# Attention decode on one core: the product with V turned to 512 moving columns in four column tiles

## The chip, the cores and the metric

The kernel runs on one core of a Trainium2 chip. The metric is the device time of one execution in microseconds (us), as the median of several executions. The time before is 677.42 us (677.16 to 677.44). A profiled execution has a span of its own, about 2 us shorter than the time.

The engines are TensorE (PE in the profile; PEld are its weight loads), VectorE (DVE), ScalarE (ACT), GpSimd (POOL) and SyncE (SP), which issues nearly all transfers. Sixteen DMA engines move the data.

## The reference

One decode step for two sequences: layer norm, 32-head attention over a cache of 8192 keys, a residual, and a gated feed-forward block. Nearly all bytes are the two caches, 134 MB each.

```python
q = (layernorm(x) @ wq)                        # 2 sequences, 32 heads, 128 wide
scores = einsum("bhqd,bhkd->bhqk", q, k) * 128 ** -0.5
p = softmax(scores)
o = einsum("bhqk,bhkd->bhqd", p, v)            # this product is what is changed
h = x + o @ wo
out = h + reglu(layernorm(h))                  # W_up, W_gate, W_down
```

## The kernel before

The work goes in 32 "pairs": one pair is two heads of one sequence. A pair has a 4 MB tile of K and a 4 MB tile of V, each 128 partitions by 128 key columns (index `j`) by 128. Head 0 sits on partitions 0 to 63, head 1 on 64 to 127. Two slots hold K tiles and two hold V tiles, so a tile is asked for two pairs ahead, as soon as its slot is free.

Scores of key columns 0 to 95 are made on VectorE (multiply, then a tree of additions), in two parts of 48. Columns 96 to 127 are transposed on TensorE, copied out by ScalarE and multiplied with q on TensorE. ScalarE takes the exponentials. Then `pv` multiplies with V:

```python
def pv(p):
    v_t = tile((2 * p + 1) % 4)
    ...                                        # cut: column of the result, waits on older batches
    for ci, (ei, j0, j1) in enumerate(parts):
        pe.wait(t_exp[p][ei], (sem_vl[ci], 16) if p == NP - 1 else t_v[p])
        for j in range(j0, j1):
            i = nc.tensor.matmul(
                Op[k % 2][:, col:col + 2], lhsT=v_t[:, j, :], rhs=e_t[p % 2][:, j, :],
                start=(nmm == 0), stop=(nmm == J - 1))
            nmm += 1
    t_pv[p] = pe.run(i)
```

V is the stationary operand, 128 x 128 for each `j`, and the two columns of exp weights (one for each head, zero on the other head's partitions) move. That is 128 weight loads and 128 matmuls a pair.

The loop over pairs, cut:

```python
for p in range(NP):
    for c in range(NCH):                       # the two VectorE parts
        dve.wait(t_k[p])                       # K tile has landed, on all DMA engines
        ...                                    # cut: multiply, tree of adds
        if c == 0:
            pe.wait(t_k[p])
            ...                                # cut: transposes, copies, score matmuls, exp
    sp.wait(*t_kfree[p])                       # both engines have read the K tile
    t_k[p + 2] = load(s, slot[s][:], kv(A_k_cache, p + 2))
    pv(p)
    load_v(p + 2)                              # waits for t_pv[p]
```

At the end `pv(30)`, the normalization of pairs 24 to 30, most of the output projection and then `pv(31)` follow. The last V tile arrives in four parts, and 48 matmuls of `pv(31)` wait for its late parts. After them come scale, the last of the output projection and the feed-forward block.

The softmax here doesn't subtract the row's maximum and nothing guards it: scores larger than these inputs give would overflow.

## Time and profile before

| | before |
|---|---|
| time, us | 677.42 |
| span of the profiled run, us | 675.6 |
| busy, us: PE / DVE / ACT | 294.0 / 493.6 / 202.0 |
| moved | 281 MB at 417 GB/s |
| instruction packets in the TensorE queue (q8) | 51 |

First the head of the page of the kernel before: busy time by engine, then the span in 40 slices (DMA row: mean busy share of the 16 engines in tenths), then the queues (packets, MB, share of the time of 16 engines).

```profile
PE 294.0 (44%) x6596; PEld 266.2 (39%) x6596; DVE 493.6 (73%) x428; ACT 202.0 (30%) x523; POOL 1.7 (0%) x11
...
DMA  9999999999999999999999999999999999999993
GB/s 373 433 434 370 430 426 432 427 430 428 434 427 430 430 434 429 432 434 427 424 428 430 431 432 434 429 432 430 426 429 428 431 428 433 428 430 392 418 411 117
...
q1 hardware_dynamic: 15872, 281.06, 97.9%
q8 instruction: 51, 0.84, 0.5%
q14 instruction: 9, 0.07, 0.0%
```

An instruction packet is one transfer that brings part of the program itself to an engine; q8 carries TensorE's (51 packets, 0.84 MB, so 16 KB each), q14 those of other engines.

No compute engine is close to full, and the DMA row is full until the last slice. Next the costly groups of the same page: line, engine, operation, tiles, count, then busy us and mean ns of one, then the idle time before and what ended it.

```profile
L366 DVE TENSOR_TENSOR prod<-slot,q_b 128x6144 bf16<-128x6144 bf16 x64 | 214.9, 3358 | 132.3 <-DMA slot<-in_A_k_cache_dram 131.1
L334 PE MATMUL O<-e,slot 128*128 128x2 bf16 x4096 | 118.7, 165 | 239.2 <-DMA slot<-in_A_v_cache_dram 119.8
L334 PEld LDWEIGHTS O<-e,slot 128*128 128x128 bf16 x4096 | 114.6, 104 | 243.5 <-ACT e L267 122.0
```

VectorE waits 131.1 us for K tiles. The chain of waits of the kernel before shows their rhythm. Its columns are the start, the length and what it was; start plus length is when a K tile had landed, and every second tile shows.

```profile
165.97 27.69 DMA slot<-in_A_k_cache_dram
...
204.81 27.86 DMA slot<-in_A_k_cache_dram
...
243.83 29.06 DMA slot<-in_A_k_cache_dram
...
284.06 27.70 DMA slot<-in_A_k_cache_dram
```

They land at 193.66, 232.67, 272.89 and 311.76 us, so 39.0, 40.2 and 38.9 us apart.

The end of the kernel before, from its timeline (start, length, engine, what, then the idle time before it and what ended it):

```profile
648.23 3.55 PE L334 MATMUL O<-e,slot 128*128 128x2 bf16 x128
...
664.30 1.44 PE L334 MATMUL O<-e,slot 128*128 128x2 bf16 x48 [1.55 <-DMA slot<-in_A_v_cache_dram]
```

The first line is a whole pair's PV, 3.55 us. The second is the 48 matmuls that wait for the last V part; TensorE idled 1.55 us before them, and 11.3 us of dependent work follow.

### The profile page before, as it was taken

The numbers are of one execution on the slowest core, as the hardware profiler recorded it, in microseconds if no ns is written. First come the engines' busy times: TensorE is split into PE (matmuls) and PEld (weight loads), VectorE is DVE, ScalarE is ACT, GpSimd is POOL, SyncE is SP. The second block draws the span as 40 slices with busy tenths as digits, with TensorE's granted clock in tenths as the row PEclk, the third lists the DMA queues.
The fourth block names the chain that finished last, engine by engine and source line by source line (L and its number), as shares of the span: only waits on it lengthen the run. The fifth ranks groups of instructions, "written<-read, shape, count | busy, mean of one in ns | idle before, by whom it ended". The sixth has DMA issues, their size and how long they took to land.

```text
span 675.6 us, 14430 instructions
## 1 busy us (share of the span) xinstructions
PE 294.0 (44%) x6596; PEld 266.2 (39%) x6596; DVE 493.6 (73%) x428; ACT 202.0 (30%) x523; POOL 1.7 (0%) x11
## 2 busy tenths in 40 slices
PE   2552254344445424443533444353344644334446
PEld 2442244333434423443433444343344534334335
DVE  1774577788777768877767887776788767778891
ACT  0630322233333223333312333331233332223330
POOL 1000000000000000000000000000000000000000
PEclk9955655566655566556556556555556555556555
DMA  9999999999999999999999999999999999999993
GB/s 373 433 434 370 430 426 432 427 430 428 434 427 430 430 434 429 432 434 427 424 428 430 431 432 434 429 432 430 426 429 428 431 428 433 428 430 392 418 411 117
DMA packets 15936, 281.97 MB, mean 417 GB/s; under 512 B 1442, under 2 KB 6916, under 8 KB 7044
## 3 DMA queue, kind: packets, MB, share of 16 engines
q1 hardware_dynamic: 15872, 281.06, 97.9%
q8 instruction: 51, 0.84, 0.5%
q14 instruction: 9, 0.07, 0.0%
q10 hardware_dynamic: 4, 0.00, 0.0%
HBM read 281.05 MB, written 0.00 MB: 416 GB/s over the span
## 4 chain that ended last, share of the span: by engine, by line
DMA 73%; DVE 24%; PE 1%; issue 1%; SPq 0%; DVEq 0%
DMA slot<-in_A_k_cache_dram 69%; DVE prod L366 15%; DVE tb L374 5%; DMA slot<-in_A_v_cache_dram 4%; DVE prod L374 3%; DVE scores L381 1%; PE S L473 0%; PE O L515 0%; PE O L334 0%; SPq L353 0%; SPq L135 0%; SPq L428 0%; PE W L473 0%; PE O L473 0%; PE W L309 0%
## 5 line engine op out<-in xcount | busy, mean ns | idle before, releaser
L366 DVE TENSOR_TENSOR prod<-slot,q_b 128x6144 bf16<-128x6144 bf16 x64 | 214.9, 3358 | 132.3 <-DMA slot<-in_A_k_cache_dram 131.1
L334 PE MATMUL O<-e,slot 128*128 128x2 bf16 x4096 | 118.7, 165 | 239.2 <-DMA slot<-in_A_v_cache_dram 119.8
L334 PEld LDWEIGHTS O<-e,slot 128*128 128x128 bf16 x4096 | 114.6, 104 | 243.5 <-ACT e L267 122.0
L397 ACT ACTIVATE kT<-T 128x1024 bf16<-128x1024 bf16 x128 | 126.5, 1022 | 170.6 <-PE T L391 169.7
L391 PE MATMUL T<-ident,slot 128*128 128x128 bf16 x1024 | 122.6, 306 | 77.5 <-DMA slot<-in_A_k_cache_dram 75.2
L374 DVE TENSOR_TENSOR tb<-prod 128x3072 bf16<-128x3072 bf16 (+1 forms) x128 | 148.2, 1158 | 4.4
L391 PEld LDWEIGHTS T<-ident,slot 128*128 128x128 bf16 x1024 | 99.7, 141 | 80.5 <-DMA slot<-in_A_k_cache_dram 78.2
L267 ACT ACTIVATE e<-scores 64x48 bf16<-64x48 f32 x128 | 32.8, 256 | 253.2 <-DVE scores L381 251.6
L374 DVE TENSOR_TENSOR prod<-tb 128x1536 bf16<-128x1536 bf16 (+1 forms) x128 | 84.2, 658 | 4.4
L259 PE MATMUL S<-qT,kT 128*128 128x2 bf16 x1024 | 48.2, 168 | 39.0 <-ACT kT L397 37.8
L259 PEld LDWEIGHTS S<-qT,kT 128*128 128x128 bf16 x1024 | 40.8, 107 | 57.6 <-ACT kT L397 57.6
L381 DVE TENSOR_REDUCE scores<-prod 128x48 f32<-128x384 bf16 x64 | 35.4, 553 | 2.2
L267 ACT ACTIVATION_READ_ACCUMULATOR e<-scores 64x1 f32 x128 | 23.6, 185 | 0.0
L267 ACT ACTIVATE e<-S 64x32 bf16<-64x32 f32 x64 | 12.9, 202 | 15.0 <-PE S L259 14.2
L267 ACT ACTIVATION_READ_ACCUMULATOR e<-S 64x1 f32 x64 | 12.9, 201 | 0.7
L212 DVE CAST qT<-W 128x64 bf16<-128x64 f32 x1 | 0.2, 225 | 12.0 <-PE W L207 12.0
L241 ACT ACTIVATE q_b<-O 128x512 bf16<-128x512 f32 x8 | 4.3, 595 | 15.6 <-PE O L236 15.6
L309 PE MATMUL W<-O_sb,X 128*128 128x2 bf16 (+1 forms) x136 | 5.0, 172 | 7.0 <-DVE O_sb L297 7.0
L309 PEld LDWEIGHTS W<-O_sb,X 128*128 128x128 bf16 x136 | 4.8, 118 | 7.2 <-DVE O_sb L297 7.2
L207 PE MATMUL W<-xlT,X 128*128 128x2 bf16 x128 | 3.6, 165 | 8.6 <-DMA X<-in_A_wq_dram 8.6
L207 PEld LDWEIGHTS W<-xlT,X 128*128 128x128 bf16 x128 | 3.5, 104 | 8.7 <-DMA X<-in_A_wq_dram 8.7
L285 DVE TENSOR_REDUCE zr<-O 128x16 f32<-128x48 f32 (+1 forms) x4 | 0.8, 204 | 8.3 <-PE O L277 8.3
(58 smaller groups left out, 39.3 us busy)
## 6 DMA issues: line engine op xcount, KB each, us to landing
slot<-in_A_k_cache_dram SPq DMA_DIRECT2D x32, 4096.0 KB, 27.8
slot<-in_A_v_cache_dram SPq DMA_DIRECT2D x31, 4096.0 KB, 32.2
X<-in_A_wq_dram SPq DMA_DIRECT2D x1, 4096.0 KB, 12.4
X<-in_A_wo_dram SPq DMA_DIRECT2D x1, 4096.0 KB, 49.1
slot<-in_A_v_cache_dram SPq DMA_DIRECT2D x1, 1536.0 KB, 21.5
slot<-in_B_W_up_dram SPq DMA_DIRECT2D x1, 1376.0 KB, 9.8
slot<-in_B_W_gate_dram SPq DMA_DIRECT2D x1, 1376.0 KB, 16.4
slot<-in_A_v_cache_dram SPq DMA_DIRECT2D x1, 1280.0 KB, 24.1
```

What stands on the lines that cost most here:

```text
L207: i = nc.tensor.matmul(Wp[:, h * B:(h + 1) * B], lhsT=wq[:, c, h * Dh:(h + 1) * Dh], rhs=lT[:, c * B:(c + 1) * B], start=(c == 0), stop=(c ...
L241: t_cp[m] = act.run(nc.scalar.activation(out=q_b[:, m * 512:(m + 1) * 512], in_=Op[m % 2][:], func=ACT.Copy))
L259: i = nc.tensor.matmul(Sp[p % 2][:, 2 * jj:2 * jj + 2], lhsT=kT[n % 3][:, k * 128:(k + 1) * 128], rhs=qT[:, 2 * p:2 * p + 2], start=True, ...
L267: t = act.run(nc.scalar.activation(out=e_t[p % 2][q, j0:j0 + nj, a], in_=src(q, a), func=ACT.Exp, scale=inv_sqrt_dh, accum_out=zs[q, 2 * p ...
L285: dve.run(nc.vector.tensor_reduce(out=zr[:, 2 * p0:2 * p1], in_=zbank(k)[:, 64:64 + n * (NCH + 1)].rearrange("p (n k) -> p n k", k=NCH + 1 ...
L309: i = nc.tensor.matmul(Wp[:, c * B + b0:c * B + b1], lhsT=wo_m[:, h, c, :], rhs=Ov[:, h // 2, h % 2, b0:b1], start=first[0], stop=last, sk ...
L334: i = nc.tensor.matmul(Op[k % 2][:, col:col + 2], lhsT=v_t[:, j, :], rhs=e_t[p % 2][:, j, :], start=(nmm == 0), stop=(nmm == J - 1))
L366: t_dm = dve.run(nc.vector.tensor_tensor(out=prod[:], in0=k_t[:, c * JC:(c + 1) * JC, :], in1=qv, op=ALU.mult))
L374: dve.run(nc.vector.tensor_tensor(out=o, in0=cur[:, :, 0:half], in1=cur[:, :, half:w], op=ALU.add))
L381: t_s = dve.run(nc.vector.tensor_reduce(out=sc[:], in_=cur, axis=AX.X, op=ALU.add))
L391: i = nc.tensor.transpose(Tp[n % 3][:, k * 128:(k + 1) * 128], k_t[:, j, :], ident[:])
L397: t_ev[n] = act.run(nc.scalar.activation(out=kT[n % 3][:], in_=Tp[n % 3][:], func=ACT.Copy))
```

## The change

The intent: swap the operands. Eight columns of exp weights (four key columns of two heads) become the stationary operand, and four key columns of V, 512 wide, move. That makes 32 matmuls a pair instead of 128. They go in turn to four column tiles of the array, which can work side by side. The result is an 8 x 512 block in each tile, of which only the "diagonal" blocks (exp column of `j` with V of the same `j`) are wanted. ScalarE copies the bank to fp32 memory, and four small fp32 matmuls with a selection matrix add the wanted blocks. The last pair keeps the old form.

```diff
-                        for j in range(j0, j1):
+                        ...                    # last pair: as before
+                        for j in range(j0, j1, VJ):           # VJ = 4
+                            g = 32 * (nmm % 4)
                             i = nc.tensor.matmul(
-                                Op[k % 2][:, col:col + 2], lhsT=v_t[:, j, :], rhs=e_t[p % 2][:, j, :],
-                                start=(nmm == 0), stop=(nmm == J - 1))
+                                o[g:g + 2 * VJ, :], lhsT=e_t[p % 2][:, j:j + VJ, :].rearrange("p j a -> p (j a)"),
+                                rhs=v_t[:, j:j + VJ, :].rearrange("p j d -> p (j d)"),
+                                start=(nmm < 4), stop=(nmm >= J // VJ - 4))
                             nmm += 1
...
+                def collect(p):                # run in the next pair, after its first exp
+                    act.wait(t_pv[p])
+                    ...
+                    t_os[p] = act.run(nc.scalar.activation(out=os_sb[:], in_=Op[p % 2][:], func=ACT.Copy))
+                    ...
+                    for jj in range(VJ):
+                        i = nc.tensor.matmul(
+                            Ob[:, 2 * p:2 * p + 2], lhsT=os_sb[:, jj * Dh:(jj + 1) * Dh],
+                            rhs=sel[:, 2 * jj:2 * jj + 2], start=(jj == 0), stop=(jj == VJ - 1))
...
-        Tp = [ps(f"T{i}", [128, GT * 128], BF16) for i in range(3)]
+        Tp = [ps(f"T{i}", [128, GT * 128], BF16) for i in range(2)]
...
+                            if p == NP - 1 and c == 1 and w == Dh // 2:
+                                t_O[3] = normalize(3, 24, 31, t_batch[3], False)
```

Cut here: the selection matrix built on GpSimd, the zeroing of the two banks, and the bookkeeping of batches. The results need a bank of their own (`Ob`), so the transposes give one up. The normalization of pairs 24 to 30 moves into VectorE's work of the last pair.

More of the change, by code (lines that the diff above doesn't have):

```diff
@@ L66, in bass_sequential_preLN__gqa_block_cached__glu_gated_reglu__decode_kernel @@
     FR = F - 10 * 128
+    VJ = 4
     eps = 1e-5
@@ L126, in bass_sequential_preLN__gqa_block_cached__glu_gated_reglu__decode_kernel @@
         o_c = sb("o_c", [128, B * DC], BF16)
-        Tp = [ps(f"T{i}", [128, GT * 128], BF16) for i in range(3)]
+        os_sb = sb("os_sb", [128, 512], F32)
+        sel = sb("sel", [128, VJ * 2], F32)
+        Tp = [ps(f"T{i}", [128, GT * 128], BF16) for i in range(2)]
         Sp = [ps(f"S{i}", [128, 512], F32) for i in range(2)]
         Op = [ps(f"O{i}", [128, 512], F32) for i in range(2)]
+        Ob = ps("Ob", [128, 512], F32)
         Wp = ps("W", [128, 512], F32)
@@ L166, in _ @@
                 pool.run(nc.gpsimd.memset(onesn[:], 1.0 / D))
+                pool.run(nc.gpsimd.memset(sel[:], 0.0))
+                for c in range(4):
+                    pool.last()
+                    pool.run(nc.gpsimd.tensor_copy(
+                        out=sel[32 * c:32 * c + 2 * VJ, :], in_=ident_f[0:2 * VJ, 0:2 * VJ]))
+                pool.last()
                 for e in e_t:
@@ L242, in _ @@
                         out=q_b[:, m * 512:(m + 1) * 512], in_=Op[m % 2][:], func=ACT.Copy))
+                dve.wait(t_cp[NP // 4 - 2], t_cp[NP // 4 - 1])
+                for o in Op:
+                    t_zero = dve.run(nc.vector.memset(o[:], 0.0))
                 t_pt, t_ev, t_sc, t_pv = {}, {}, {}, {}
+                t_os, t_ob = {}, {}
                 t_exp = {}
@@ L272, in zbank, with zcol @@
                 def zbank(k):
-                    return Sp[0] if k == 4 else Op[k % 2]
+                    return Sp[0] if k == 4 else Ob
+                def zcol(k):
+                    return 64 if k == 4 else 2 * NP
                 def z_sum(k, p0, p1):
@@ L277, in z_sum @@
                     t = pe.run(nc.tensor.matmul(
-                        zbank(k)[:, 64:64 + (p1 - p0) * 2 * (NCH + 1)], lhsT=ones_f[:],
+                        zbank(k)[:, zcol(k):zcol(k) + (p1 - p0) * 2 * (NCH + 1)], lhsT=ones_f[:],
                         rhs=zs[:, 2 * p0:2 * p1, :], start=True, stop=True))
@@ L286, in normalize @@
                         out=zr[:, 2 * p0:2 * p1],
-                        in_=zbank(k)[:, 64:64 + n * (NCH + 1)].rearrange("p (n k) -> p n k", k=NCH + 1),
+                        in_=zbank(k)[:, zcol(k):zcol(k) + n * (NCH + 1)].rearrange("p (n k) -> p n k", k=NCH + 1),
                         axis=AX.X, op=ALU.add))
@@ L296, in o_scale @@
                 def o_scale(k, p0, p1):
+                    src = Op[1][:, 0:2] if k == 4 else Ob[:, 2 * p0:2 * p1]
                     return dve.run(nc.vector.tensor_tensor(
-                        out=O_sb[:, 2 * p0:2 * p1], in0=Op[k % 2][:, 0:2 * (p1 - p0)], in1=zi[:, 2 * p0:2 * p1],
+                        out=O_sb[:, 2 * p0:2 * p1], in0=src, in1=zi[:, 2 * p0:2 * p1],
                         op=ALU.mult))
@@ L323, in pv @@
                     v_t = tile((2 * p + 1) % 4)
-                    k = next(kk for kk, (a, b_) in enumerate(batches) if a <= p < b_)
-                    col = 2 * (p - batches[k][0])
+                    o = Op[p % 2]
                     parts = vparts if p == NP - 1 else (
                         [(0, NCH * JC, J)] + [(1 + c, c * JC, (c + 1) * JC) for c in range(NCH)])
-                    if p == batches[k][0] and k >= 2:
-                        pe.wait(t_O[k - 2])
+                    pe.wait(t_zero)
+                    if p >= 2:
+                        pe.wait(t_os[p - 2])
                     nmm = 0
@@ L332, in pv @@
                         pe.wait(t_exp[p][ei], (sem_vl[ci], 16) if p == NP - 1 else t_v[p])
-                        for j in range(j0, j1):
+                        if p == NP - 1:
+                            for j in range(j0, j1):
+                                i = nc.tensor.matmul(
+                                    o[:, 0:2], lhsT=v_t[:, j, :], rhs=e_t[p % 2][:, j, :],
+                                    start=(nmm == 0), stop=(nmm == J - 1))
+                                nmm += 1
+                            continue
+                        for j in range(j0, j1, VJ):
+                            g = 32 * (nmm % 4)
                             i = nc.tensor.matmul(
-                                Op[k % 2][:, col:col + 2], lhsT=v_t[:, j, :], rhs=e_t[p % 2][:, j, :],
-                                start=(nmm == 0), stop=(nmm == J - 1))
+                                o[g:g + 2 * VJ, :], lhsT=e_t[p % 2][:, j:j + VJ, :].rearrange("p j a -> p (j a)"),
+                                rhs=v_t[:, j:j + VJ, :].rearrange("p j d -> p (j d)"),
+                                start=(nmm < 4), stop=(nmm >= J // VJ - 4))
                             nmm += 1
                     t_pv[p] = pe.run(i)
-                    if p + 1 in ends and p < NP - 1:
+                def collect(p):
+                    act.wait(t_pv[p])
+                    if p >= 1:
+                        act.wait(t_ob[p - 1])
+                    t_os[p] = act.run(nc.scalar.activation(out=os_sb[:], in_=Op[p % 2][:], func=ACT.Copy))
+                    k = next(kk for kk, (a, b_) in enumerate(batches) if a <= p < b_)
+                    pe.wait(t_os[p])
+                    if p == batches[k][0] and k >= 1:
+                        pe.wait(t_O[k - 1])
+                    for jj in range(VJ):
+                        i = nc.tensor.matmul(
+                            Ob[:, 2 * p:2 * p + 2], lhsT=os_sb[:, jj * Dh:(jj + 1) * Dh],
+                            rhs=sel[:, 2 * jj:2 * jj + 2], start=(jj == 0), stop=(jj == VJ - 1))
+                    t_ob[p] = pe.run(i)
+                    if p + 1 in ends:
                         t_batch[k] = z_sum(k, *batches[k])
@@ L361, in _ @@
                         dve.wait(t_k[p])
-                        if p == 0 and c == 0:
-                            dve.wait(t_cp[NP // 4 - 1])
                         dve.last()
@@ L386, in _ @@
                                 n = p * NG + g
-                                if n >= 3:
-                                    pe.wait(t_ev[n - 3])
+                                if n >= 2:
+                                    pe.wait(t_ev[n - 2])
                                 for k in range(GT):
@@ L391, in _ @@
                                     i = nc.tensor.transpose(
-                                        Tp[n % 3][:, k * 128:(k + 1) * 128], k_t[:, j, :], ident[:])
+                                        Tp[n % 2][:, k * 128:(k + 1) * 128], k_t[:, j, :], ident[:])
                                 t_pt[n] = pe.run(i)
@@ L397, in _ @@
                                 t_ev[n] = act.run(nc.scalar.activation(
-                                    out=kT[n % 3][:], in_=Tp[n % 3][:], func=ACT.Copy))
+                                    out=kT[n % 3][:], in_=Tp[n % 2][:], func=ACT.Copy))
                                 if g >= 1:
@@ L406, in _ @@
                                 NCH * JC, JP)
+                            if p == NP - 1:
+                                pv(p - 1)
+                            if p >= 1:
+                                collect(p - 1)
                         act.wait(t_s)
@@ L434, in _ @@
                             B_W_down[0:10 * 128].rearrange("(r p) n -> p r n", p=128)).then_inc(sem_wd, 16)
-                pv(NP - 2)
-                t_O[3] = normalize(3, 24, 31, t_batch[3], False)
                 pe.wait(t_O[3])
```

## The prediction

> **What bounds the kernel now.** The DMA queue. In the page's slices the 16 DMA engines are at least 90% busy in every slice but the last; 281 MB move at 417 GB/s over a 675.6 us span. In the chain of waits K tiles land 38.9 us apart for two pairs: 19.43 us per pair of 4 MB K and V tiles, 432 GB/s. VectorE (73% busy) waits 131.1 us for K tiles, about 4 us a pair; TensorE (44%) and ScalarE (30%) wait for VectorE or DMA. The queue is deep: by the list of DMA issues a V tile lands 32.2 us after its issue, against 9.7 us for moving one. So a V slot may come free some 20 us later (estimate: 32.2 less a tile or so) before the queue runs dry.
>
> **What the change does to TensorE.** PV is now 128 matmuls a pair with 2 moving columns: in the timeline 80 in 2.27 us and 48 in 1.44 us, 3.7 us. After: 32 matmuls of 512 columns. The 128-column transposes run 8 in 1.01 us, 1 ns a column, so 32 x 512 columns in series would take 13 to 16 us (estimate). If the column tiles overlap as the Trainium skill ("TensorE: Matmul & The Clock Gate", Part 3) measured, 2.38 times for three, it is 4 to 5.5 us (estimate). No gain for TensorE. Added per pair: one 128x512 fp32 eviction on ScalarE (595 ns for that shape at start-up, 18 us in all) and 4 fp32 matmuls (the fp32 sum of ones shows as two passes, 0.25 us of weight load each), about 2 us. Two transpose buffers instead of three cost nothing: the score group already waits for the same eviction. All off the critical path.
>
> **What is on it.** The DMA stream, then the end: the last V part lands at 664.25 us; 48 unchanged matmuls, scale, output projection and feed-forward take 11.3 us more. Before that landing TensorE idles 1.55 us, and the moved third normalization only spends 0.6 us of VectorE earlier. The bubble near 618 us (392 GB/s in its slice), where the last K tile's issue waits for VectorE, stays.
>
> One small gain: instruction fetch shares the DMA engines. The page counts 51 instruction packets, 0.84 MB, 16 KB each, which agrees with the Trainium skill ("Runtime: NRT & Kernel Launch", Instruction fetch mechanics: blocks of 16 KiB, 256 instructions). Their 0.5% of 16 engines is about 3.4 us. TensorE loses 31 x (256 - 64 - 16) = 5456 instructions, 21 packets: about 1.4 us of DMA time (estimate). I expect most of it to show.
>
> **Prediction.** 676.3 us, 8 in 10 between 675.2 and 677.7. Faster by over 2%: 0.01; within 2%: 0.97; slower by over 2%: 0.02.
>
> **What would show it.** DMA busy share still 9 in all slices but the last; instruction packets near 30; PV's TensorE time 4 to 6 us a pair (over 10: the tiles do not overlap); ScalarE busy about 220 us; VectorE's the same; the last V landing about 1 us earlier, and 11.3 us from there to the end.
>
> **What would make it wrong.** Column tiles in series at the low clock: about 22 us of TensorE per pair against 19.43, over 2% slower; or the last pair's longer chain (PV 30, eviction, sums, normalization inside VectorE's chain) ending after the last V landing, 1 to 7 us more; or fetches that were hidden, so no gain.

## The result, and the profile after

| | before | after |
|---|---|---|
| time, us, median (range) | 677.43 (677.16 to 677.45) | 672.79 (672.58 to 673.44) |
| ratio (95% interval) | | 0.9935 (0.9921 to 0.9949) |
| span of the profiled run, us | 675.6 | 670.7 |
| instructions in the span | 14430 | 8986 |
| last V part landed, us | 664.25 | 659.30 |

Ratios in this document are the mean time of one kernel's fast runs over that of the other's of the same rounds, so they are not quite the ratio of the medians quoted beside them.

The change is 4.6 us faster. I had forecast 1.1 us, with a range that ended at 675.2: the sign was right, the size was not. The page of the changed kernel, the same lines as before:

```profile
PE 352.0 (52%) x3868; PEld 234.1 (35%) x3868; DVE 494.4 (74%) x430; ACT 220.1 (33%) x554; POOL 2.5 (0%) x16
...
DMA  9999999999999999999999999999999999999994
GB/s 375 434 436 357 434 435 430 427 431 429 434 433 427 428 433 433 425 436 425 434 433 427 431 436 424 431 432 431 437 426 425 434 432 433 426 430 431 428 409 146
...
q1 hardware_dynamic: 15872, 281.06, 98.4%
q8 instruction: 30, 0.49, 0.3%
q14 instruction: 9, 0.07, 0.0%
```

TensorE is now busier (352.0 us against 294.0), not less busy, and so is ScalarE. What went down is the instruction packets of TensorE, from 51 to 30. The groups of the changed kernel:

```profile
L407 DVE TENSOR_TENSOR prod<-slot,q_b 128x6144 bf16<-128x6144 bf16 x64 | 214.9, 3358 | 128.2 <-DMA slot<-in_A_k_cache_dram 126.9
L361 PE MATMUL O<-slot,e 128*8 128x512 bf16 x992 | 116.3, 621 | 143.4 <-ACT e L282 127.8
L361 PEld LDWEIGHTS O<-slot,e 128*8 128x8 bf16 x992 | 24.0, 106 | 209.6 <-ACT e L282 155.6
```

VectorE's wait for K tiles is 4.2 us shorter in all (126.9 us), with its work the same. The chain of waits of the changed kernel, for the same stretch:

```profile
164.68 27.70 DMA slot<-in_A_k_cache_dram
...
206.31 25.98 DMA slot<-in_A_k_cache_dram
...
243.44 27.69 DMA slot<-in_A_k_cache_dram
...
282.29 27.70 DMA slot<-in_A_k_cache_dram
```

The landings are at 192.38, 232.29, 271.13 and 309.99 us, so 39.9, 38.8 and 38.9 us apart. There is again one long step, but it is 1.0 us too long and not 1.3. Over the K tiles that land between 75 and 628 us, the kernel before has five steps that are 1.4 to 1.6 us too long; the changed kernel has six, of only 0.5 to 1.1 us. (Just before the transfer that starts at 206.31 the chain runs through TensorE and ScalarE, where a batch is collected. This did not make the tile late: its first part was done at 228.93 us, 9.71 us after that of the tile before, as for the tiles around it; only its last part was late.) The end of the changed kernel, from its timeline:

```profile
645.00 3.58 PE L361 MATMUL O<-slot,e 128*8 128x512 bf16 x32
...
659.34 1.44 PE L354 MATMUL O<-e,slot 128*128 128x2 bf16 x48 [0.25 <-DMA slot<-in_A_v_cache_dram]
```

A whole pair's PV takes 3.58 us, as long as before. From the start of the 48 matmuls to the end of the span are 11.34 us (670.68 less 659.34), against 11.33 before. So nothing was gained after the last landing; the landings themselves came earlier.

**Where the landings come from.** A transfer here counts as landed when 16 completion records have come in, one from each DMA engine. The Trainium skill says so in "DMA: Bandwidth & Descriptors", section "Why a DMA increments its semaphore by 16 and not by 1": a DMA "runs on up to 16 SDMA engines that finish independently, and the semaphore counts them". The traces agree in the count: there are 16 records for each tile. They do not name the engine, so in what follows a record is taken for an engine, and which engine it is stays unknown. Sorted, in us after the first of the 16, for the K tile of pair 29:

```
before   0  0.05 0.06 0.16 0.37 0.64 3.14 4.17 7.93 7.95 8.34 9.39 9.42 9.45 9.47 9.74   first at 598.08
after    0  0.12 0.21 0.26 0.27 0.58 2.78 4.00 4.62 4.66 4.68 4.80 4.91 5.14 5.35 6.38   first at 598.14
```

The first engine is done at the same time in both kernels. Eight engines are late, by 7.9 to 9.7 us before and by 4.6 to 6.4 us after, and the tile waits for the last of them. Two more are late by about 3 and 4 us in both kernels. In the kernel before, the spread between first and last grows from 1.97 us for the K tile that lands at 75.55 us to 9.74 us here: 7.77 us, five times 1.55 us, while 40 packets of TensorE came, five for each of eight engines.

Behind each instruction packet there is one slow data packet in the records, which starts within 0.02 us of its end. Between 75 and 600 us the kernel before has 48 instruction packets (40 of TensorE's, 8 of others) and 48 data packets above 1.5 us, where the median is 1.216 us; they average 1.72 us. In the changed kernel it is 30 (22 and 8) and again 30, of 1.72 us. So a TensorE packet costs the DMA engine it lands on 1.07 us of its own and 0.50 us on a neighbour packet, 1.57 us in all. (That both fall on one engine is inferred; the spread, which grows by 1.55 us for every eight packets, agrees.) The 8 other packets fit the two engines that are late in both kernels: with the data packet behind them four cost 0.98 us each and four 0.69 to 0.72, so 3.9 and 2.8 us if each four fell on one engine (estimate).

That gives **theory F**. TensorE's instruction packets fall on eight of the sixteen DMA engines. Each puts its engine 1.57 us behind, the engine does not catch up as the next transfer is already waiting for it, and tiles land with the most delayed engine. 21 packets fewer over 8 engines are 2.6 for each, 4.1 us (estimate); as an engine gets whole packets, three fewer are 4.7 us. The rivals are **P**, that the PV form itself gains (less weight traffic, or PV done at another time), and **S**, my forecast, that packets cost their own time spread over 16 engines, 21 x 1.07 / 16 = 1.4 us.

### The profile page after: what moved, and what is told of

It reads as the page before. It is cut to its first block, busy times and chain, and to the rows that moved or that the text cites. A ratio compares the mean times of both kernels' runs of the same rounds, so it can differ in the third digit from the quotient of the medians.

```text
span 670.7 us, 8986 instructions
## 1 busy us (share of the span) xinstructions
PE 352.0 (52%) x3868; PEld 234.1 (35%) x3868; DVE 494.4 (74%) x430; ACT 220.1 (33%) x554; POOL 2.5 (0%) x16
## 4 chain that ended last, share of the span: by engine, by line
DMA 72%; DVE 22%; PE 3%; ACT 2%; issue 1%; SPq 0%; DVEq 0%
DMA slot<-in_A_k_cache_dram 68%; DVE prod L407 14%; DVE tb L415 4%; DMA slot<-in_A_v_cache_dram 3%; DVE prod L415 2%; ACT kT L440 1%; DVE scores L424 1%; PE T L434 1%; PE Ob L378 1%; ACT e L282 0%; PE S L274 0%; ACT os_sb L372 0%; PE Ob L295 0%; PE S L518 0%; PE O L560 0%
## 5 line engine op out<-in xcount | busy, mean ns | idle before, releaser
L407 DVE TENSOR_TENSOR prod<-slot,q_b 128x6144 bf16<-128x6144 bf16 x64 | 214.9, 3358 | 128.2 <-DMA slot<-in_A_k_cache_dram 126.9
L361 PE MATMUL O<-slot,e 128*8 128x512 bf16 x992 | 116.3, 621 | 143.4 <-ACT e L282 127.8
L361 PEld LDWEIGHTS O<-slot,e 128*8 128x8 bf16 x992 | 24.0, 106 | 209.6 <-ACT e L282 155.6
L378 PE MATMUL Ob<-sel,os_sb 128*128 128x2 f32 x248 | 57.5, 354 | 47.7 <-ACT os_sb L372 47.7
L378 PEld LDWEIGHTS Ob<-sel,os_sb 128*128 128x128 f32 x248 | 54.9, 327 | 51.2 <-ACT os_sb L372 51.2
L372 ACT ACTIVATE os_sb<-O 128x512 f32<-128x512 f32 x31 | 18.5, 597 | 3.4 <-PE O L361 2.7
```

The source lines that it names most:

```text
L361: i = nc.tensor.matmul(o[g:g + 2 * VJ, :], lhsT=e_t[p % 2][:, j:j + VJ, :].rearrange("p j a -> p (j a)"), rhs=v_t[:, j:j + VJ, :].rearrang ...
L372: t_os[p] = act.run(nc.scalar.activation(out=os_sb[:], in_=Op[p % 2][:], func=ACT.Copy))
L378: i = nc.tensor.matmul(Ob[:, 2 * p:2 * p + 2], lhsT=os_sb[:, jj * Dh:(jj + 1) * Dh], rhs=sel[:, 2 * jj:2 * jj + 2], start=(jj == 0), stop= ...
L407: t_dm = dve.run(nc.vector.tensor_tensor(out=prod[:], in0=k_t[:, c * JC:(c + 1) * JC, :], in1=qv, op=ALU.mult))
```

## The experiments

Nine kernels were run, in five rounds each (a_pad2 and a_less have four times on record), beside the kernel before on the same chip. One caution: a run is called right by a comparison with the reference, and a kernel below that leaves out half of V for 31 of 32 pairs passed it. The attention output is small beside the residual, so that comparison says nothing of PV. That the changed PV and the variants built on it are right rests on the code.

### a_pad1: give TensorE its instructions back

```diff
+                def pad():
+                    for _ in range(94):
+                        nc.tensor.matmul(Wp[0:8, 256:258], lhsT=ident[:, 0:8], rhs=qT[:, 0:2], start=True, stop=True)
...
                         pv(p)
+                        if p < 29:
+                            pad()
```

> The changed kernel plus 94 tiny matmuls (8 stationary, 2 moving columns, result not used) after PV of each of the pairs 0 to 28: 2726 more weight loads and 2726 more matmuls, so that TensorE has as many instructions as before the change; PV stays 512 wide. Theory F (instruction fetch delays half of the DMA engines, and the most delayed one sets when a tile lands): instruction packets back from 30 to about 51, and with them the whole gain gone: 677.4 us, 676.9 to 677.9, ratio to before 1.000; the 16 engines of the last K tiles end about 9.7 us apart again instead of 6.4. Rival P (the gain comes from PV itself: less weight traffic or an earlier end of PV): the pads fall in idle TensorE time and read few weights, so 672.8 us, ratio 0.993. Rival S (my forecast: fetch time spread over 16 engines): 674.2 us.

Measured: 677.73 us (677.63 to 677.86), before 677.33 in the same rounds, ratio 1.0005 (0.9993 to 1.0018). The whole gain is gone, and the packets are those of the kernel before. The page of this run:

```profile
PE 416.3 (62%) x6594; PEld 307.6 (46%) x6594; DVE 494.4 (73%) x430; ACT 220.6 (33%) x554; POOL 2.5 (0%) x16
...
q8 instruction: 51, 0.84, 0.5%
```

PV is still 512 wide, the pads load 8 weight columns, and 51 packets are back. The K tile of pair 29 is first done at 598.07 us and last at 608.00. P and S are out for this run, except for a P by which any TensorE work between pairs costs.

### a_pad2: twice the pads

```diff
-                    for _ in range(94):
-                        nc.tensor.matmul(Wp[0:8, 256:258], lhsT=ident[:, 0:8], rhs=qT[:, 0:2], start=True, stop=True)
+                    for _ in range(188):
+                        nc.tensor.matmul(Wp[:, 256:258], lhsT=ident[:], rhs=qT[:, 0:2], start=True, stop=True)
```

> The same with 188 pads a pair and 128 stationary columns: 5452 more weight loads and matmuls, about 42 packets more than the changed kernel has. Theory F: 42 packets over 8 engines, 5.3 more for the most delayed one at 1.55 us each, about 8 us over the changed kernel: 681 us, 680 to 682.5, ratio 1.005. Rival P: at most as slow as before the change, 673 to 677 us. Rival S: 42 x 1.07 / 16 = 2.8 us, 675.6 us.

Measured: 682.70 us, ratio 1.0080 (1.0067 to 1.0094); 73 packets. This is 0.2 us above the range of F, and it is not a clean dose. In its chain of waits TensorE holds a large share:

```profile
PE 39%; DMA 30%; DVE 15%; ACT 9%; issue 5%; SPq 1%; DVEq 0%
```

With 72% busy, TensorE had come onto the path, and even the first engine's part of K tile 29 ended at 605.98 us, 7.8 us later than in the changed kernel. The run speaks against S (675.6 us) but cannot confirm F's size.

### a_pool: instructions for an engine that does nothing

```diff
                 t_const = pool.run(nc.gpsimd.memset(zs[:], 0.0))
+                for i in range(5456):
+                    nc.gpsimd.wait_ge(sem_x, 16)
```

The build puts two of these waits into one instruction, so 2728 instructions are added and not 5456, as I had written. They all wait for a value that has been reached and constant.

> The changed kernel, TensorE untouched, plus 5456 instructions on the idle GpSimd (two satisfied waits in each of them), issued from its start. Theory F: if these are fetched over the same engines, 16 KB at a time as TensorE's are, 21 more packets and back to about 677 us (675.5 to 678); if they come over other engines or in another size, less, and the spread of the engines shows which: between 672.8 and 677. Rival P: TensorE is the same and GpSimd idle, so 672.8 us. Rival S: 674.2 us.

Measured: 681.18 us (680.58 to 681.49), ratio 1.0054 (1.0040 to 1.0068): 8.4 us slower than the changed kernel, with TensorE's work untouched. The size was off my range; the profile shows why. The page of this run:

```profile
PE 351.3 (52%) x3868; PEld 233.0 (34%) x3868; DVE 494.4 (73%) x430; ACT 220.8 (32%) x554; POOL 2.5 (0%) x16
...
q8 instruction: 30, 0.49, 0.3%
q14 instruction: 30, 0.25, 0.1%
```

The added instructions come as 21 packets of 8 KB in another queue. The 16 completions of the K tile that lands at 282.22 us, in us after the first:

```
a_pool   0  0.02 0.21 0.30 0.66 1.18 1.59 1.63 1.68 1.73 1.81 1.90 2.07 3.08 3.26 14.35
```

One single engine is 11 us behind the next. Each of the added packets takes 0.33 us and its neighbour data packet 1.57 us instead of 1.22, so 0.68 us, and 21 of them are 14.3 us: the delay fits if all fell on this one engine. The spread grows tile by tile while these packets come, to 14.3 us for the tile that lands at 243.35 us; the last of them starts at 238.60 us, and up to the tile that lands at 389.04 us the spread then stays between 14.3 and 14.4 us. The time grows by less, 8.4 us, since the changed kernel already waited for an engine that was 6.4 us late: K tile 29 lands at 612.41 us instead of 604.52. So 0.18 MB, less than a thousandth of the bytes, cost more than 1% of the time. This settles that instruction fetch alone, without any change to TensorE, ScalarE or VectorE, delays the tiles, and that what counts is the most delayed engine.

### a_serial: the four column tiles in series

```diff
-                            g = 32 * (nmm % 4)
+                            g = 0
...
-                                start=(nmm < 4), stop=(nmm >= J // VJ - 4))
+                                start=(nmm == 0), stop=(nmm == J // VJ - 1))
```

> The changed kernel with all 32 PV matmuls of a pair in one column tile instead of four (result still right, same instruction count). PV then takes 32 times 0.21 to 0.43 us, 7 to 14 us a pair, instead of 3.6. Theory F: nothing in the stream of K and V tiles moves (K tiles as far apart as in the changed kernel); only the last pairs' chain before the last V landing grows, so 674 to 682 us, all of the growth after 645 us of the trace. My forecast's fear: TensorE over 19.4 us a pair, over 690 us. Rival P: anything above 673 us with K tiles landing later all along.

Measured: 675.84 us (675.55 to 677.27), ratio 0.9983 (0.9971 to 0.9996), so 3 us slower than the changed kernel. The stream did not move: K tile 29 landed at 604.45 us (604.52 in the changed kernel) and the last V part at 659.19 (659.30). PV of pair 30, from this run's timeline and from a window over it (the number after the busy times is the granted clock, then DMA share and GB/s):

```profile
644.92 8.72 PE L361 MATMUL O<-slot,e 128*8 128x512 bf16 x32
```

```profile
645.00:653.60 8.60, 8.60 (x32) 2.91 (x32) 7.19 (x6) 0.81 (x4) 0.00 (x0) 0.81 1.00 421
```

The same 32 matmuls took 3.58 us in four tiles at a granted clock of 0.50 and 8.72 us in one tile at 0.81: there the first eight started 0.43 us apart at clock 0.50, and from 648.30 us, at 1.00, the weight loads of the last 23 took 4.84 us, 0.21 us each. So the four tiles do overlap, and almost fully: in the changed kernel's timeline a group of four starts every 0.43 us, and back-to-back matmuls of 512 columns are given a distance of 426.7 ns at the low clock by the Trainium skill ("TensorE: Matmul & The Clock Gate", Part 1). 32 in series at 0.43 us would take 13.8 us (estimate), 3.8 times as long as the four tiles took. Part 3 of that page measured 2.38 times for three tiles. But in the stream the overlap is worth nothing. It saves only in the last pair, where a longer PV of pair 30 delays VectorE's normalization and the chain behind it past the last landing.

### b_half and b_half_pad: the old form with half the matmuls, and with its instructions restored

```diff
-                        for j in range(j0, j1):
+                        step = 1 if p == NP - 1 else 2
+                        for j in range(j0, j1, step):
                             i = nc.tensor.matmul(
                                 Op[k % 2][:, col:col + 2], lhsT=v_t[:, j, :], rhs=e_t[p % 2][:, j, :],
-                                start=(nmm == 0), stop=(nmm == J - 1))
-                            nmm += 1
+                                start=(nmm == 0), stop=(nmm == J - step))
+                            nmm += step
```

The second kernel has this and 68 pads (128 stationary columns) after PV of the pairs 0 to 28.

> The kernel before with every second PV matmul left out for the pairs 0 to 30 (wrong result on purpose): 64 instead of 128, 3968 TensorE instructions fewer, nothing of the change in it. Theory F: 15 to 16 instruction packets fewer (about 35), 15.5 / 8 x 1.55 = 3.0 us: 674.4 us, 673.6 to 675.2, ratio 0.9956. Rival P (the 512-wide form itself, or its place in the last pair, makes the gain): 677.4 us.

> The same with 68 tiny matmuls put in after PV of the pairs 0 to 28, so that TensorE has its 51 packets of instructions again (wrong result on purpose, V read half as much). Theory F: 677.4 us, 676.8 to 678. A rival by which TensorE's reads of V slow the DMA's writes: 674.4 us, as without the pads.

Measured: b_half 674.44 us, ratio 0.9958 (0.9945 to 0.9972), 36 packets. b_half_pad 677.26 us, ratio 1.0001 (0.9989 to 1.0014), 51 packets. From the pages of the two, b_half first:

```profile
PE 240.5 (36%) x4612; PEld 212.9 (32%) x4612; DVE 493.6 (73%) x428; ACT 201.9 (30%) x523; POOL 1.7 (0%) x11
...
q8 instruction: 36, 0.59, 0.4%
```

```profile
PE 294.2 (44%) x6584; PEld 266.6 (39%) x6584; DVE 493.6 (73%) x428; ACT 202.2 (30%) x523; POOL 1.7 (0%) x11
...
q8 instruction: 51, 0.84, 0.5%
```

Both are within 0.2 us of F. Nothing of the change is in either kernel, so the gain needs no 512-wide matmul, only fewer instructions; and reading half of V, with the instruction count kept, gains nothing.

### a_less: fewer TensorE instructions still

For the pairs 0 to 28 TensorE transposes 16 key columns instead of 32, and VectorE takes 56 in each part instead of 48.

```diff
+    NGP = [2 if p < 29 else NG for p in range(NP)]           # groups of 8 key columns on TensorE
+    JCP = [(J - g * GT) // NCH for g in NGP]                 # key columns in each VectorE part
...                                                           # and their use for JC, NG and the buffers
```

> The changed kernel with the score work of the pairs 0 to 28 moved: TensorE transposes 16 instead of 32 of the 128 key columns, VectorE takes 56 instead of 48 in each of its two parts (right result). TensorE loses 1856 instructions, 7 packets (30 to 23); VectorE gains about 2.6 us a pair, of its 4 us of idle time. Theory F: 7 / 8 x 1.55 = 1.4 us less than the changed kernel: 671.4 us, 670.8 to 672.3, ratio to before 0.991. A rival by which VectorE or TensorE time counts in the stream: slower than 673 us.

Measured: 671.42 us (671.31 to 671.59), ratio 0.9914 (0.9901 to 0.9928). The page of this run:

```profile
PE 291.8 (44%) x2940; PEld 173.8 (26%) x2940; DVE 558.1 (83%) x430; ACT 161.7 (24%) x496; POOL 2.5 (0%) x16
...
q8 instruction: 23, 0.38, 0.2%
```

VectorE got 64 us more work, the time fell by 1.4 us against the changed kernel (across two jobs, each beside its own runs of the kernel before), as F said. The step is small: the intervals of the two ratios (0.9901 to 0.9928 and 0.9921 to 0.9949) just overlap, while the ranges of the times do not. Of the kernels that are meant to keep the result right, this one is the fastest here.

### a_less_bal and a_less_bal2: give the late engines less to carry

If eight engines are late, they could be given fewer data packets. Both kernels are a_less with a tile loaded in pieces, some of them of only 8 partitions.

```diff
+        def load_bal(s, dst, src):                            # a_less_bal: K of pair 31, V of pair 30
+            for a, b_ in ((0, 112), (112, 120), (120, 128)):
+                t = load(s, dst[a:b_, :], src[a:b_, :])
+            return t
```

```diff
+        def load_bal(s, dst, src):                            # a_less_bal2: V of pair 26
+            w = 96 * Dh
+            load(s, dst[:, 0:w], src[:, 0:w])
+            for i in range(16):
+                t = load(s, dst[i:128:16, w:], src[i:128:16, w:])
+            return t
```

> The kernel a_less, with the last K tile and the last but one V tile loaded in three transfers, of 112, 8 and 8 partitions, instead of one of 128 (right result). By the Trainium skill (DMA: Bandwidth & Descriptors, Why a DMA increments its semaphore by 16 and not by 1) a transfer of 8 partitions runs on the lowest-numbered 8 of the 16 engines; those then move 9 packets of 32 KB of each of the two tiles and the other 8 move 7, at 1.21 us a packet in the traces. Theory F: eight engines are 4 to 5 us late at the end. If they are the upper eight, they are relieved of 2 x 1.21 = 2.4 us and the last V landing comes that much earlier: 669.1 us, 668.5 to 669.8. If they are the lower eight, they get 2.4 us more: 673.8 us. If the late engines lie in both halves, 671.5 to 674. A rival by which the lateness is of the queue as a whole and not of single engines: 671.4 us, unchanged.

> The kernel a_less with the V tile of pair 26 loaded as one transfer of its first 96 key columns for all 128 partitions and 16 transfers of the other 32 columns, each for 8 partitions that lie 16 apart (right result). The lower 8 engines (the Trainium skill, DMA: Bandwidth & Descriptors, Why a DMA increments its semaphore by 16 and not by 1) then move twice the last quarter of the tile, the upper 8 none of it, 2.4 us more and less than 9.7 us. After a_less_bal, where packets of 32 KB took twice their time with 112 and 8 partitions, it is open whether these packets keep their rate. If they do and the late engines are the upper eight: 669.0 us, 668.3 to 670. If they do and the late ones are the lower eight: 673.9 us. If these packets slow down too, by 1.5 or 2 times in this one tile, 674 to 685 us, and the landing times of single engines tell no more than that.

Measured: a_less_bal 701.74 us (699.01 to 703.89), ratio 1.0362 (1.0338 to 1.0385); a_less_bal2 680.48 us (680.01 to 681.28), ratio 1.0048 (1.0034 to 1.0061). Both lost. Two windows of a_less_bal, before and during the split tiles (granted clock, DMA share and GB/s are the last three numbers):

```profile
590.00:610.00 20.00, 9.55 (x102) 5.48 (x102) 17.81 (x15) 5.97 (x16) 0.00 (x0) 0.59 1.01 434
618.00:632.00 14.00, 6.03 (x68) 4.21 (x68) 5.56 (x3) 4.26 (x8) 0.00 (x0) 0.50 1.01 218
```

That a transfer of 8 partitions uses eight engines agrees with the trace: K tile 31 has 34 completion records here where a whole tile has 16, which fits 16, 9 and 9 (eight engines, and one record for those left out). All 16 engines are busy throughout, but the rate is halved: data packets of 32 KB take about 2.4 us instead of 1.21. In a_less_bal2 the same happens from 547 to 560 us, also to packets of the ordinary transfers beside. So the runs do not tell which eight engines are late, and nothing was learned of balancing. Why the packets slow down when the engines work on differently cut transfers stays open.

### The runs side by side

For each profiled run: instruction packets of TensorE, when the first and the last of the 16 engines had finished K tile 29, when the last V part had landed, and the span, in us.

```
run          packets   K29 first   K29 last   last V    span
before           51      598.08     607.82    664.25    675.6
a_pad1           51      598.07     608.00    664.49    675.7
b_half_pad       51      598.03     607.53    663.70    675.2
b_half           36      597.96     604.97    661.28    672.8
after            30      598.14     604.52    659.30    670.7
a_serial         30      598.08     604.45    659.19    673.7
a_less           23      598.05     603.02    658.13    669.5
a_pad2           73      605.98     612.75    669.39    680.7
a_pool           30      599.38     612.41    667.64    679.4     (and 21 more of GpSimd's)
```

The engine that finishes first does so at 598.1 us in the first seven, whatever TensorE does. In the last two it is later too: in a_pad2 TensorE was on the path, and in a_pool one request, issued at 374.00 us after a late landing and a batch's normalization, came 1.3 us too late for the engines that were on time. In the first seven the last follows the count of packets, from 9.5 to 9.9 us behind at 51 to 5.0 at 23. From the last V landing to the end of the span are 11.3 to 11.8 us, but for a_serial with its longer end.

The mean of the eight late engines tells the price of a packet without the packet records. At K tile 29 they are 3.87 us behind the first when 18 TensorE packets have come by 598 us (a_less), 5.07 us at 25 (after), 6.39 us at 30 (b_half) and 8.96 us at 44 (before): 8 x (8.96 - 3.87) / (44 - 18) = 1.57 us a packet, the same as above.

## Why the prediction was right or wrong

- **What bounds the kernel: half right.** It is the DMA stream, and no compute engine. But "the DMA queue" is not one thing. At K tile 29 the 16 engines finish 9.7 us apart, and the slowest one is the bound.
- **PV's cost: right, a little too high.** I said 4 to 6 us a pair if the tiles overlap, and no gain for TensorE; it is 3.6 to 3.8 us (a burst of 20 in 2.31 us and one of 12 in 1.45), against 3.55 to 3.7. ScalarE rose to 220.1 us (I said about 220), VectorE stayed (493.6 to 494.4), and the end after the last landing stayed at 11.3 us.
- **Tiles in series: wrong.** I feared over 2% slower, at 22 us of TensorE a pair. The run with one tile lost 3 us, all at the end. The low clock that I multiplied with did not stay in that run: it was 0.81 in the window above and 0.78 over the run, against 0.62 in the changed kernel.
- **The bubble near 618 us: a wrong reading.** I took the slice with 392 GB/s for time lost that stays. In the window from 617.5 to 619.5 us of the kernel before, the DMA share is 0.72: six of the 16 engines had finished K tile 30 by 618.15 us, and the next K tile was only asked for at 618.98. The ten others are still carrying earlier tiles, and the late ones are the bound. In the changed kernel that slice moves 431 GB/s.
- **Instruction fetch: the right cause, and the count exact (30 packets), but the cost of a packet was wrong.** The failing step reads: "TensorE loses 31 x (256 - 64 - 16) = 5456 instructions, 21 packets: about 1.4 us of DMA time (estimate)." I spread a packet's own time of 1.07 us evenly over 16 engines. The runs show 8 engines, 1.57 us a packet and the most delayed engine as the bound: 21 / 8 x 1.57 = 4.1 us, or 4.7 for three whole packets. Measured were 4.6 us in the time and 4.95 us in the last V landing.
- **"The last V landing about 1 us earlier": wrong by the same term.** The K tile of pair 29 landed 3.30 us earlier (two whole packets are 3.1 us), the last V part 4.95 (three are 4.7).

In the page the clue was there: the odd 40.2 us in a rhythm of 38.9, and a share of 0.5% that is an average over 16 engines of a load that only some of them carry.

What stays open: why TensorE's packets would go to eight engines and GpSimd's to one (both inferred from the landings), which engines these are, and why the data packet beside an instruction packet takes 0.5 us longer.

## What to carry to other kernels

When a kernel is bound by transfers that are spread over all DMA engines, look at the spread of the completions of one tile, not only at the mean busy share: the tile lands with the slowest engine, and a small load on few engines can set it. Here the instruction count of TensorE was such a load, at 1.5 to 1.8 us for every eight packets of 256 instructions (2.8 us for 15 packets, 4.6 for 21, 5.9 for 28); fewer and larger instructions, or work moved to an engine with long instructions, shortened a kernel whose engines all had time to spare. Any change that alters the number of instructions should be compared with a padded version before its gain is put down to what it computes.

## What the Trainium skill lacked or had wrong

- "Runtime: NRT & Kernel Launch", Instruction fetch mechanics, says that instructions come in 16 KiB blocks of 256, and that the cost of crossing a block is "mostly hidden". The size agrees for TensorE (51 packets, 0.84 MB). The cost was not hidden in this kernel, which is bound by DMA: 21 blocks fewer were 4.6 of 677.4 us.
- No page says that instruction packets are unevenly spread over the DMA engines: by the landings TensorE's fell on eight of sixteen (8 to 10 us late), GpSimd's on one (11 us behind the next). A packet of 16 KB cost its engine 1.57 us, of which 0.50 us on a neighbouring data packet.
- "Runtime: NRT & Kernel Launch", Instruction fetch mechanics, also implies blocks of 16 KiB for every engine; GpSimd's came as 8 KB packets (21 for 2728 instructions).
- "TensorE: Matmul & The Clock Gate", Part 3, gives a measured gain of column packing for three tiles (2.38 times) and none for four. Four tiles of 8 x 512 here ran 32 matmuls in 3.58 us at clock 0.50, a group of four every 0.43 us.
- "DMA: Bandwidth & Descriptors" tells how many engines a transfer of 8 or 112 partitions uses, and its rules ask for 128 partitions for the most bandwidth, which I passed over. No page gives what such pieces cost in a stream of whole tiles. Here the rate was halved: 32 KB packets took about 2.4 us instead of 1.21, and 218 GB/s moved instead of 434.
